# Moving the first k products forward in the first chunk of a q, k, v projection

## The chip, the cores and the metric

The kernel runs on one core of a Trainium2 chip. The metric is the device time of one execution in microseconds (us); the time before is the median of three runs, and the time after will be compared with it as a ratio. The engines are named as the profile names them: PE is TensorE (matmuls), PEld its weight loads, ACT is ScalarE, DVE is VectorE, POOL is GpSimd, and SP is SyncE, which here issues all the DMAs, one after the other.

## The reference

The inputs are a sequence x of 2048 tokens with 448 features, and weights. Everything is fp32. Cut to what matters:

```python
qkv = x @ wqkv                                # 448 -> 3 * 448, split into q, k, v of 16 heads x 28
# head h, position s: 8 keys at s, s-2, ..., s-14 (positions below 0 masked)
attn = softmax(q . k * 28**-0.5)              # over those 8
a = (attn . v) @ wo
b = relu(x @ w1 + b1)**2 @ w2 + b2            # 448 -> 1792 -> 448
g = sigmoid((x * gate_w).sum(-1))
out = g * a + (1 - g) * b
```

## The kernel before, in words

**Splitting for precision.** Every fp32 operand of a matmul is split into a high part (a rounded copy, made by ACT) and a low part (the operand minus the high part, made by DVE); `split_full` does both. A product then takes three matmuls: high x high, high x low, low x high. The q weights' parts are `wqh` and `wql`, which also hold the k and v weights in later columns.

**Row tiles.** The 448 features on the contracted side are three row tiles of 128 and a last one of 64. `full` lists the products of the row tiles named to it for one tile of 128 tokens; `last` lists those of the 64 rows. The last row tile of q and that of k lie in the two halves of one 128-row tile, `w7h`/`w7l`.

**Half-height pairs.** From `run` on, PE works in pairs: `side_by_side` (matmul at L186) issues two matmuls, one on array rows 0 to 63 and one on rows 64 to 127, for two different accumulators. A full product of 128 rows is thus issued once in each half, at different times. When an accumulator changes from one half to the other, `turn` puts a one-element write into its PSUM bank, on DVE (a 1x1 memset, L196) or, where one accumulator turns alone, on ACT (L194). PE waits for it before it goes on with that accumulator in the other half.

**Chunks.** The tokens come in four chunks of 512, each of four tiles of 128. The first chunk is done by `qkv_first`, the others by `qkv_two`, two token tiles at a time. In `qkv_first`, PE begins with q: for each of the three full row tiles in turn, twelve full-height matmuls (L255), four token tiles x three terms. Then comes the half-height part: q's last rows beside k's last rows, k's full row tiles, and then v. k's four accumulators take PSUM banks with the tag "m", those of q and then of v take banks with the tag "b".

**Loads at the start.** SP issues, in this order: for each row tile the q weights and the first chunk's tokens (tile `rx`; those of the first row tile in two halves), then the last row tile, then the three k weights, the three v weights, the last v rows (`raw7`), and the second chunk's tokens. These last take the buffer of the q weights, so they wait until DVE has copied the gate's weights out of it (L674). Thirteen matmuls on zeros (L634) run before the first tokens are there.

**Evacuation and storing.** `qkv_evacuate` (L205, ACT) copies an accumulator into a staging tile `st` that holds two token tiles; when both are in, SP stores it (L211) to `q_d`, `k_d` or `v_d` in HBM. The pool of staging tiles has three buffers (`ST_BUFS`). In the first chunk the first two hold q, the third and the fourth hold k, and the next two v.

**What sets the order.** The program is written once, with a planner's clock that stands for PE's time: each group of matmuls calls `advance` with an estimated cost (`MM448` = 203 ns for one matmul or one pair), and work registered with a due time is emitted at the first `advance` that passes it. In `run`, `advance` is called in steps of up to twelve pairs, and evacuations and turns are emitted behind it. Around the first chunk the due times are: storing the first chunk's split tokens to `x_d` (`x_spill`, four stores at L142) at 10,500; splitting the v weights at 12,000, 12,900, 13,800 and 14,700; the gate's partial products on DVE from 15,000; splitting the second chunk's tokens from 19,000. Each engine executes its instructions in the order in which they were emitted; only the waits between engines are settled at run time.

**Later.** From the second chunk on, attention runs on POOL and DVE beside PE's projections and then beside the two matmuls of the dense part.

Of the kernel before, what the change touches and what calls it, by code (L numbers as in the profile page):

```python
# [7 lines left out]
F32 = mybir.dt.float32  # L8
# [5 lines left out]
S, D, H, DH, W, F = 2048, 448, 16, 28, 8, 1792  # L14
P = 128
# [42 lines left out]
def gated_mix_kernel(ctx: ExitStack, tc: tile.TileContext, xT, wqkv, w1, w2, wo, b1, b2, out):  # L58
    nc = tc.nc

    def f32(ap):
        return ap.bitcast(F32)
# [30 lines left out]
    attp = ctx.enter_context(tc.tile_pool(name="attp", bufs=1))  # L93
# [20 lines left out]
    def split_full(raw, hi, lo, soon=now):  # L114
        nc.scalar.activation(hi, raw, AF.Copy)
        soon(lambda: nc.vector.tensor_sub(lo, raw, f32(hi)))

    def split_x78(raw, x7, x8, soon=now):

        split_full(raw, x7, x8, soon)  # L120
# [12 lines left out]
    def x_tiles(c, pool):  # L133
        return X([pool.tile([P, 2, CH], F32R, tag=f"x{j}", name=f"x{c}_{j}") for j in range(4)])
# [19 lines left out]
    wqh = ap.tile([P, 3, NP + 2 * D], F32R, name="wqh")  # L154
    wql = ap.tile([P, 3, NP + 2 * D], F32R, name="wql")
# [10 lines left out]
    def block(b):  # L166

        o = (0, NP, NP + D)[b]
        return slice(o, o + D)
# [43 lines left out]
    def full(x, acc, tl, b, ks=range(3)):  # L213
        sl, n = slice(tl * P, tl * P + P), block(b)
        r = []
        for k in ks:
            r += [(acc, x.h[k][:, sl], wqh[:, k, n]), (acc, x.h[k][:, sl], wql[:, k, n]),
                  (acc, x.l[k][:, sl], wqh[:, k, n])]
        return r

    def last(x, acc, tl, b):

        sl = slice(tl * P, tl * P + P)
        n = block(1) if b == 2 else slice(0, D)
        h, l = w7h[:, n], w7l[:, n]
        return [(acc, x.x7[:, sl], h), (acc, x.x7[:, sl], l), (acc, x.x8[:, sl], h)]

    def accs(c, b, tls, tags):
        return [Acc(t, f"qkv{c}_{tl}_{b}", D) for t, tl in zip(tags, tls)]

    def run(c, todo, steps):


        a = 0
        for e, done, *turns in steps:
            side_by_side(todo[0][a:e], todo[1][a:e])
            while a < e:
                advance(min(12, e - a) * MM448)
                a = min(a + 12, e)
            for t in turns:  # L240
                t() if callable(t) else turn(*t)
            for b, tl, acc in done:
                assert acc.todo == 0
                qkv_evacuate(acc.pt, c, tl, b)

    def qkv_first(x):


        four = range(4)
        q = accs(0, 0, four, "bbbb")  # L250
        for k in range(3):
            for two in ((0, 1), (2, 3)):
                for j, prods in enumerate(zip(*(full(x, q[i], i, 0, (k,)) for i in two))):
                    for acc, a, w in prods:
                        nc.tensor.matmul(acc.pt[:, :D], a, w, start=k == j == 0, stop=False)  # L255
            advance(12 * MM448)
        for acc in q:
            acc.todo = 3
        k = accs(0, 1, four, "mmmm")
        t = [sum((last(x, a[i], i, b) for i in four), []) for b, a in ((0, q), (1, k))]  # L260
        f = [full(x, k[i], i, 1) for i in four]
        run(0, [t[0] + f[0] + f[1] + f[2] + f[3], t[1] + f[2] + f[3] + f[0] + f[1]],
            [(3, [(0, 0, q[0])], (k[0], k[0])),
             (12, [(0, i, q[i]) for i in (1, 2, 3)], (k[1], k[1])),
             (24, [], (k[0], k[2])), (33, [], (k[1], k[3])),
             (39, [(1, 0, k[0]), (1, 2, k[2])]), (48, [(1, 1, k[1]), (1, 3, k[3])])])
        v = accs(0, 2, four, "bbbb")
        f, l = [full(x, v[i], i, 2) for i in four], [last(x, v[i], i, 2) for i in four]
        run(0, [f[0] + l[0] + f[2] + l[2] + f[1] + f[3], f[1] + l[1] + f[3] + l[3] + f[0] + f[2]],
            [(15, [], (v[0], v[1])), (24, [], (v[2], v[3])),  # L270
             (33, [(2, 0, v[0]), (2, 1, v[1])]), (42, [(2, 2, v[2]), (2, 3, v[3])])])
# [201 lines left out]
    def soon(fn):  # L473
        at(LO_DELAY, fn)

    def advance(dt):
        clock["pe"] += dt
        while due := [x for x in later if x[0] <= clock["pe"]]:
            item = min(due, key=lambda x: x[0])
            later.remove(item)  # L480
            item[1]()
        if not clock["on"]:
            clock["att"] = clock["pe"]
            return
        while clock["att"] < clock["pe"]:
            try:
                r = next(att)
            except StopIteration:
                clock["on"] = False
                return  # L490
            if r is None:
                clock["att"] = clock["pe"]
                return
            clock["att"] += r


    def raw_tile(name):
        return rawp.tile([P, 4, 512], F32, tag="raw", name=name)
# [94 lines left out]
    def h_first(x, c, f):  # L593

        accs = [Acc("m", f"h{c}_{f + r}", CH) for r in range(2)]
        go([h_last(x, a, f) + h_full(x, a, f + r, (0, 1, 2)) for r, a in enumerate(accs)], MM512)
        return accs
# [38 lines left out]

    raws = [raw_tile("wqraw0")]
    rx = raw_tile("xraw0")
    for k in range(4):
        if k < 3:  # L640
            nc.sync.dma_start(raws[0][:, k, :NQ], wqkv[0, :, k])
        else:
            for b, rows in ((0, slice(0, 64)), (1, slice(64, P))):
                nc.sync.dma_start(raws[0][rows, k, :NQ], wqkv[b, rows, k])
        for cols in ((slice(0, 256), slice(256, CH)) if k == 0 else (slice(0, CH),)):
            nc.sync.dma_start(rx[:, k, cols], xT[0, :, k, cols])

    for b, tag in ((1, "k"), (2, "v")):
        raw = attp.tile([P, 3, D], F32, tag=tag, name=f"wqraw{b}")
        for k in range(3):  # L650
            nc.sync.dma_start(raw[:, k], wqkv[b, :, k, :D])
        raws.append(raw)
    raw7 = attp.tile([P, D], F32, tag="q", name="wqraw7")
    nc.sync.dma_start(raw7, wqkv[2, :, 3, :D])
    x = x_tiles(0, xap)
    for k in range(3):
        nc.scalar.activation(wqh[:, k, :D], raws[0][:, k, :D], AF.Copy)
        halves = (slice(0, 256), slice(256, CH))
        for i, cols in enumerate(halves):

            if k == i == 0:
                nc.vector.tensor_copy(x.h[k][:, cols], rx[:, k, cols])
            else:
                nc.scalar.activation(x.h[k][:, cols], rx[:, k, cols], AF.Copy)
        nc.vector.tensor_sub(wql[:, k, :D], raws[0][:, k, :D], f32(wqh[:, k, :D]))
        for cols in halves:
            nc.vector.tensor_sub(x.l[k][:, cols], rx[:, k, cols], f32(x.h[k][:, cols]))
    split_full(raws[0][:, 3, :D], w7h[:, :D], w7l[:, :D])
    split_x78(rx[:, 3], x.x7, x.x8)

# [36 lines left out]
    def wq_split(b, k):  # L707
        if k < 3:
            split_full(raws[b][:, k], wqh[:, k, block(b)], wql[:, k, block(b)])
        else:  # L710
            split_full(raw7, w7h[:, NP:], w7l[:, NP:])
# [34 lines left out]
        nc.sync.dma_start(b1t, b1)  # L746
        nc.sync.dma_start(b2t, b2.partition_broadcast(P))

    for k in range(3):
        wq_split(1, k)  # L750
    for k in range(4):
        when(12000.0 + k * 900.0, wq_split, 2, k)
# [40 lines left out]
    for c in range(4):  # L793
        x = xs[c]
        if c == 0:
            qkv_first(x)
        else:
            qkv_two(x, c, 0, copies=c == 3)
            qkv_two(x, c, 2, (mlp_one, mlp_two) if c == 3 else (), c == 3)
        if c == 1:  # L800
            st_["spilled"] = 0
            clock["on"] = True
            clock["att"] = clock["pe"] - 1.0
            advance(0.0)
        if c == 3:
            st_["spilled"] = 1
# [282 lines left out]
    c, x = ORDER[0], xm[3]  # L1089
# [8 lines left out]
    for g in range(2, 2 * NF):  # L1098
        i, f = g // (NF // 2), g % (NF // 2) * 2
# [4 lines left out]
        if not f:  # L1104
            x, slots = X([nxt[j][0] for j in range(4)]), [nxt[j][1] for j in range(4)]
            nxt = {}
        hold[0] = ends
        accs = h_first(x, c, f)
# [112 lines left out]
```

## Time and profile before

| | us |
|---|---|
| time, median of 3 runs | 413.13 (412.95 to 413.48) |
| the profiled execution: time | 413.8 |
| the profiled execution: span, first to last instruction | 412.0 |
| PE busy | 407.8 |
| DVE busy | 270.6 |
| ACT busy | 210.4 |
| POOL busy | 268.4 |

The profile's page counts as busy the time in which an engine has an instruction in work. Matmuls are pipelined and their ends are modelled, so that two matmuls overlap in the rows and PE's real pace is read from start to start. A row of the timeline merges neighbouring instructions of one kind; its second column is then the time from the first start to the last end. Times of rows count from the span's start.

### The profile page before, as it was taken

The numbers are of one execution on the slowest core, as the hardware profiler recorded it, in microseconds if no ns is written. First come the engines' busy times: TensorE is split into PE (matmuls) and PEld (weight loads), VectorE is DVE, ScalarE is ACT, GpSimd is POOL, SyncE is SP. The second block draws the span as 40 slices with busy tenths as digits, with TensorE's granted clock in tenths as the row PEclk, the third lists the DMA queues.
The fourth block names the chain that finished last, engine by engine and source line by source line (L and its number), as shares of the span: only waits on it lengthen the run. The fifth ranks groups of instructions, "written<-read, shape, count | busy, mean of one in ns | idle before, by whom it ended". The sixth has DMA issues, their size and how long they took to land.

```text
span 412.0 us, 9331 instructions
## 1 busy us (share of the span) xinstructions
PE 407.8 (99%) x3835; PEld 366.0 (89%) x3835; DVE 270.6 (66%) x430; ACT 210.4 (51%) x461; POOL 268.4 (65%) x167
## 2 busy tenths in 40 slices
PE   8999999999999999999999999999999999999997
PEld 7999999999888888888888888989898888888996
DVE  4590745276767766787656798879576677892354
ACT  4641646387775555444565535444653254346540
POOL 0000001955999999989989899999899977940000
PEclk9999999999999999999999999999999999999999
DMA  7999999979262315654112649765146530168304
GB/s 213 368 351 309 286 390 288 355 223 315 91 241 99 128 51 209 208 186 152 41 47 105 222 158 270 196 146 154 28 157 200 217 130 2 45 179 132 95 0 181
DMA packets 66763, 73.83 MB, mean 179 GB/s; under 512 B 33120, under 2 KB 59296, under 8 KB 66464
## 3 DMA queue, kind: packets, MB, share of 16 engines
q1 hardware_dynamic: 66720, 73.23, 55.4%
q8 instruction: 30, 0.49, 0.5%
q14 instruction: 13, 0.11, 0.1%
HBM read 45.74 MB, written 28.28 MB: 180 GB/s over the span
## 4 chain that ended last, share of the span: by engine, by line
PE 99%; DVE 0%; issue 0%
PE b L186 33%; PE h L186 32%; PE qkv L186 23%; PE a L186 7%; PE qkv L255 2%; PE warm L634 1%; PE a L993 1%; PE last L993 0%; DVE bt L872 0%; PE last L985 0%; PE a L985 0%; DVE zero L631 0%; DVE b1z L632 0%
## 5 line engine op out<-in xcount | busy, mean ns | idle before, releaser
L335 POOL TENSOR_TENSOR qk<-q,k 128x896 f32<-128x896 f32 x64 | 135.2, 2144 | 84.2 <-DMA k<-k_d 76.0
L342 POOL TENSOR_TENSOR av<-lg,v 128x896 f32<-128x896 f32 x64 | 119.2, 1957 | 6.2 <-DVE lg L336 5.6
L621 DVE TENSOR_TENSOR h<-h,h 128x512 fp32r<-128x512 f32 x56 | 38.4, 688 | 66.8 <-ACT h L624 66.5
L186 PE MATMUL qkv<-wqh,x 64*128 64x448 f32 x528 | 78.2, 359 | 0.0
L336 DVE TENSOR_REDUCE lg<-qk 128x32 f32<-128x896 f32 x64 | 67.0, 1074 | 0.0
L350 DVE TENSOR_REDUCE o<-av 128x112 f32<-128x896 f32 x64 | 66.4, 1070 | 0.1
L186 PE MATMUL b<-w2ah,h 64*128 64x448 f32 x448 | 66.3, 359 | 0.0
L186 PE MATMUL b<-w2bh,h 64*128 64x448 f32 x448 | 66.1, 359 | 0.0
L622 ACT ACTIVATE h<-h,b1z 128x512 f32<-128x512 f32 x56 | 36.7, 655 | 43.6 <-PE h L186 43.6
L186 PEld LDWEIGHTS qkv<-wqh,x 64*128 64x128 f32 x528 | 49.4, 184 | 3.6
L186 PE MATMUL qkv<-wql,x 64*128 64x448 f32 x264 | 47.7, 358 | 0.0
L186 PEld LDWEIGHTS b<-w2bh,h 64*128 64x128 f32 x448 | 42.1, 184 | 3.5
L186 PEld LDWEIGHTS b<-w2ah,h 64*128 64x128 f32 x448 | 42.0, 184 | 3.7
L205 ACT ACTIVATE st<-qkv 128x448 f32<-128x448 f32 x48 | 23.5, 542 | 34.3 <-PE qkv L186 31.7
L186 PE MATMUL b<-w2bl,h 64*128 64x448 f32 x224 | 40.7, 358 | 0.0
L186 PE MATMUL b<-w2al,h 64*128 64x448 f32 x224 | 40.5, 358 | 0.0
L623 ACT ACTIVATE h<-h 128x512 fp32r<-128x512 f32 x56 | 33.5, 598 | 1.7
L624 ACT ACTIVATE h<-h 128x512 f32<-128x512 f32 x56 | 33.3, 594 | 0.0
L573 ACT ACTIVATE h<-h 128x4 fp32r<-128x4 f32 (+1 forms) x35 | 7.2, 207 | 44.4 <-PE b L186 44.2
L186 PE MATMUL h<-x2b,w1h 64*128 64x512 f32 x168 | 28.1, 386 | 0.0
L186 PE MATMUL h<-x,w1h 64*128 64x512 f32 x168 | 28.1, 386 | 0.0
L186 PE MATMUL h<-x1b,w1h 64*128 64x512 f32 x168 | 28.1, 386 | 0.0
(150 smaller groups left out, 688.6 us busy)
## 6 DMA issues: line engine op xcount, KB each, us to landing
k<-k_d SPq DMA_DIRECT2D x8, 840.0 KB, 5.6
v<-v_d SPq DMA_DIRECT2D x8, 840.0 KB, 5.0
x_d<-x SPq DMA_DIRECT2D x11, 512.0 KB, 6.8
q_d<-st SPq DMA_DIRECT2D x8, 448.0 KB, 5.5
k_d<-st SPq DMA_DIRECT2D x8, 448.0 KB, 5.2
v_d<-st SPq DMA_DIRECT2D x8, 448.0 KB, 5.8
w1raw<-w SPq DMA_DIRECT2D x4, 896.0 KB, 9.2
q<-q_d SPq DMA_DIRECT2D x8, 448.0 KB, 3.6
```

The costliest lines, as they stand in the source:

```text
L186: nc.tensor.matmul(acc.pt[:, :acc.n], a[rows], w[rows], start=acc.todo == acc.all, stop=acc.todo == 1)
L205: nc.scalar.activation(st[:, :, t % 2], pt[:, :D].rearrange("p (g c) -> p g c", g=G), AF.Copy)
L255: nc.tensor.matmul(acc.pt[:, :D], a, w, start=k == j == 0, stop=False)
L335: nc.gpsimd.tensor_mul(pr, q[:, s:s + 1].to_broadcast([P, W, C]), k[:, s:s + W])
L336: pending.append(lambda: nc.vector.tensor_reduce(lg[:, s], pr.rearrange("p w (h d) -> p w h d", h=HG), axis=AX.X, op=ALU.add))
L342: nc.gpsimd.tensor_mul(pr.rearrange("p (h d) w -> p w h d", h=HG), lg[:, s][:, :, :, None].to_broadcast([P, W, HG, DH]), v[:, s:s + W].rea ...
L350: nc.vector.tensor_reduce(o[:, g * C:(g + 1) * C], pr, axis=AX.X, op=ALU.add)
L573: nc.scalar.activation(ap, f32(ap), AF.Copy)
L621: nc.vector.tensor_sub(hl, pt, f32(hh))
L622: ops += [lambda pt=pt, r=r: nc.scalar.activation(pt, pt, AF.Relu, bias=b1t[:, f + r:f + r + 1]), lambda pt=pt, hh=hh: nc.scalar.activatio ...
L623: lambda pt=pt, hh=hh: nc.scalar.activation(hh, pt, AF.Square),
L624: lambda pt=pt, r=r, low=low: (nc.scalar.activation(pt, pt, AF.Square), at(delays[r], low))]
```

## The change

The first row tile of k is multiplied right behind the first row tile of q, at full height, by the loop that did q alone before. Its weights are loaded behind the first tokens and split behind the first tokens' low parts. The half-height part for k then does only row tiles 1 and 2, so that its pairs and the places of the evacuations and turns are counted anew: 36 pairs and not 48. The number of multiplications stays the same: twelve full-height matmuls take the place of twelve pairs. The k and v weights' buffers are declared earlier; the other loads keep their order among themselves.

```diff
         four = range(4)
-        q = accs(0, 0, four, "bbbb")
-        for k in range(3):
+        q, k = accs(0, 0, four, "bbbb"), accs(0, 1, four, "mmmm")
+        for b, n, acs in ((0, 0, q), (1, 0, k), (0, 1, q), (0, 2, q)):
             for two in ((0, 1), (2, 3)):
-                for j, prods in enumerate(zip(*(full(x, q[i], i, 0, (k,)) for i in two))):
+                for j, prods in enumerate(zip(*(full(x, acs[i], i, b, (n,)) for i in two))):
                     for acc, a, w in prods:
-                        nc.tensor.matmul(acc.pt[:, :D], a, w, start=k == j == 0, stop=False)
+                        nc.tensor.matmul(acc.pt[:, :D], a, w, start=n == j == 0, stop=False)
             advance(12 * MM448)
         for acc in q:
             acc.todo = 3
-        k = accs(0, 1, four, "mmmm")
+        for acc in k:
+            acc.todo = 15
         t = [sum((last(x, a[i], i, b) for i in four), []) for b, a in ((0, q), (1, k))]
-        f = [full(x, k[i], i, 1) for i in four]
+        f = [full(x, k[i], i, 1, (1, 2)) for i in four]
         run(0, [t[0] + f[0] + f[1] + f[2] + f[3], t[1] + f[2] + f[3] + f[0] + f[1]],
             [(3, [(0, 0, q[0])], (k[0], k[0])),
              (12, [(0, i, q[i]) for i in (1, 2, 3)], (k[1], k[1])),
-             (24, [], (k[0], k[2])), (33, [], (k[1], k[3])),
-             (39, [(1, 0, k[0]), (1, 2, k[2])]), (48, [(1, 1, k[1]), (1, 3, k[3])])])
+             (21, [], (k[0], k[2])), (27, [], (k[1], k[3])),
+             (30, [(1, 0, k[0]), (1, 2, k[2])]), (36, [(1, 1, k[1]), (1, 3, k[3])])])
...
     rx = raw_tile("xraw0")
+    raws += [attp.tile([P, 3, D], F32, tag=tag, name=f"wqraw{b}") for b, tag in ((1, "k"), (2, "v"))]
     for k in range(4):
...
             nc.sync.dma_start(rx[:, k, cols], xT[0, :, k, cols])
-
-    for b, tag in ((1, "k"), (2, "v")):
-        raw = attp.tile([P, 3, D], F32, tag=tag, name=f"wqraw{b}")
-        for k in range(3):
-            nc.sync.dma_start(raw[:, k], wqkv[b, :, k, :D])
-        raws.append(raw)
+        if k == 0:
+            nc.sync.dma_start(raws[1][:, 0], wqkv[1, :, 0, :D])
+
+    for b in (1, 2):
+        for k in range(b == 1, 3):
+            nc.sync.dma_start(raws[b][:, k], wqkv[b, :, k, :D])
...
             nc.vector.tensor_sub(x.l[k][:, cols], rx[:, k, cols], f32(x.h[k][:, cols]))
+        if k == 0:
+            split_full(raws[1][:, 0], wqh[:, 0, block(1)], wql[:, 0, block(1)])
...
-    for k in range(3):
+    for k in (1, 2):
         wq_split(1, k)
```

## The prediction

> **What bounds the kernel now.** First the page's busy times and the chain that ended last, then busy time by stretch (columns: stretch, sum of busy time, PE's busy time and instructions, granted clock, DMA share, GB/s).
>
> ```profile
> PE 407.8 (99%) x3835; PEld 366.0 (89%) x3835; DVE 270.6 (66%) x430; ACT 210.4 (51%) x461; POOL 268.4 (65%) x167
> ...
> 1.19 3.14 PE warm L634 x13
> 4.34 8.87 PE qkv L255 x36
> 13.21 91.55 PE qkv L186 x912
> ```
> ```profile
> 8.00:13.00 5.00, 5.00 (x26) 1.00 1.01 344
> 13.00:31.20 18.20, 18.20 (x182) 1.00 0.99 353
> 31.20:105.00 73.80, 73.80 (x740) 1.00 0.90 302
> 105.00:405.00 300.00, 300.00 (x2846) 1.00 0.44 135
> ```
>
> PE is the bound, and from 8 us to 405 us it shows no idle time at all. Two things follow. A microsecond for which PE is made to wait early on is not given back later, because there is no later wait in which it could vanish. And the change can only gain what PE loses before 13 us. That loss is read from the timeline's first matmuls (columns here and in all rows of this kind: start, time, engine, line, operation, tiles, count, and in brackets the idle time before and what ended it), from the weight loads (PEld) between them, and from the view of waits.
>
> ```profile
> 5.11 0.95 PE L255 MATMUL qkv<-wql,x 128*128 128x448 f32 x2
> 5.86 1.59 PE L255 MATMUL qkv<-wqh,x 128*128 128x448 f32 x4
> 7.29 0.56 PE L255 MATMUL qkv<-wql,x 128*128 128x448 f32 x2
> ...
> 9.84 0.56 PE L255 MATMUL qkv<-wql,x 128*128 128x448 f32 x2
> 10.25 0.96 PE L255 MATMUL qkv<-wqh,x 128*128 128x448 f32 x4
> 11.04 0.56 PE L255 MATMUL qkv<-wql,x 128*128 128x448 f32 x2
> ...
> 13.14 0.47 PE L186 MATMUL qkv<-w7h,x 64*128 64x448 f32 x2
> ```
> ```profile
> 8.13 0.30 PEld L255 LDWEIGHTS qkv<-wqh,x 128*128 128x128 f32 x2 [0.25 <-ACT x L664]
> ```
> ```profile
> PEld qkv L186 <- ACT wqh L115: 0.3, 1, 0.3
> PEld qkv L255 <- ACT x L664: 0.3, 1, 0.3
> ```
>
> In the steady part six full matmuls take 11.04 - 9.84 = 1.20 us, 0.20 us each. From 5.11 to 5.86 two of them take 0.75 us, 0.375 each, although the granted clock stands at 1.00. So of the 8.87 us of the 36 first matmuls, 36 x 0.20 = 7.2 are the work and 1.67 the loss, and most of the loss is the slow pace before 7.3 us, which the change does not touch. The one wait that more work from the first row tile can cover is the 0.25 to 0.3 us for the second tile's tokens (ACT x L664, at 8.1 us). The 0.3 at the switch to half-height matmuls (L186) stays.
>
> **The change, part by part.** *Matmuls.* Twelve full products of k (4 token tiles x 3 terms) come in behind the first 12 of q: 12 x 0.20 = 2.40 us. Out go 12 half-height pairs: 91.55 / 912 x 2 = 0.2008 us a pair, 2.41 us. Net zero. PE's own schedule becomes: half-height part from 13.14 - 0.2 + 2.4 = 15.35 us; after 36 pairs v's products; after 78 pairs the second chunk at 31.05, against 31.26 now (second pair of the last row below). That is a gain of 0.2 us, if nothing else waits.
>
> ```profile
> 30.86 0.36 PE L186 MATMUL qkv<-wql,x 64*128 64x448 f32 x2
> 31.06 0.56 PE L186 MATMUL qkv<-wqh,x 64*128 64x448 f32 x4
> ```
>
> *The first k weights.* One 224 KB transfer moves ahead of seven on SP's queue (q's second, third and last weights and the tokens between and behind them). It lands where q's second weights land today: ACT starts on those at 6.24, so k's are split at 6.24 + 0.58 = 6.8 on ACT and 0.6 later, 7.5, on DVE; PE wants them at 7.9.
>
> ```profile
> 5.62 0.42 ACT L664 ACTIVATE x<-xraw 128x256 fp32r<-128x256 f32 x1 [1.59 <-DMA xraw<-xT]
> 6.24 0.58 ACT L657 ACTIVATE wqh<-wqraw 128x448 fp32r<-128x448 f32 x1 [0.20 <-DMA wqraw<-wqkv]
> ```
>
> Those seven, and their splits, come 6.24 - 5.62 = 0.6 us later. PE now needs the second tile 2.4 us later, so all of that is covered; it would cost up to 0.6 without the new matmuls. Issue on SP (0.4 us) is not the limit, since the DMA share is about 1 already. The later k and v weights keep their place. The one follower that is not covered is the second chunk's tokens: their buffer comes free at DVE's copy of the gate's weights, now 12.0 + 0.16, then about 12.8, so they are issued and land up to 0.6 us later.
>
> ```profile
> 12.00 0.16 DVE L674 COPY zs<-wqraw 128x4 f32<-128x4 f32 x1
> ```
>
> *The queue's order, which the diff does not show.* The planner's clock reaches 10,500 ns, the due time of x_spill, in a different place. Today q's four tiles are evacuated by 9,744 (48 steps of 203) and the spill follows; changed, the first comes at 10,353 and the other three at 12,180 (60 steps), so before those three the spill's four x_d stores and one of v's weight splits are emitted first. On SP the four 512 KB x_d stores now stand ahead of the two q_d stores, and SP works strictly in order. The timeline of SP before:
>
> ```profile
> 15.34 1.45 SPq L211 DMA_DIRECT2D q_d<-st  x2
> 16.84 4.58 SPq L142 DMA_DIRECT2D x_d<-x  x4
> 23.64 0.99 SPq L211 DMA_DIRECT2D k_d<-st  x2
> ```
>
> Who waits for q_d: the pool of staging tiles has three buffers, and k's third tile (the fourth staging tile) takes the buffer of q's first. ACT's evacuation at about 21.7, second of the first row below, therefore waits until the first q_d store has landed. Today that is 15.34 + 5.5 = 20.8, under 1 us early. ACT's and DVE's rows of that stretch:
>
> ```profile
> 21.26 0.98 ACT L205 ACTIVATE st<-qkv 128x448 f32<-128x448 f32 x2 [3.00 <-PE qkv L186]
> 23.06 0.98 ACT L205 ACTIVATE st<-qkv 128x448 f32<-128x448 f32 x2 [0.82 <-PE qkv L186]
> 23.93 1.15 ACT L115 ACTIVATE x<-xraw 128x512 fp32r<-128x512 f32 x2
> ```
> ```profile
> 24.59 0.69 DVE L116 TENSOR_TENSOR x<-xraw,x 128x512 fp32r<-128x512 f32 x1 [0.18 <-ACT x L115]
> ...
> 26.28 0.06 DVE L196 MEMSET qkv<- 1x1 f32 x2
> ...
> 28.84 0.06 DVE L196 MEMSET qkv<- 1x1 f32 x2
> ```
>
> Landing of the changed order, call it T. The timeline's row of the last x_d store, and the view of DMA issues at 15.4, 20.8 and 23.8 us (tiles, count, KB, us from issue to landing):
>
> ```profile
> 20.35 1.07 SPq L142 DMA_DIRECT2D x_d<-x  x1
> ```
> ```profile
> q_d<-st SPq DMA_DIRECT2D x1, 448.0 KB, 5.5
> ```
> ```profile
> x_d<-x SPq DMA_DIRECT2D x1, 512.0 KB, 6.7
> ```
> ```profile
> k_d<-st SPq DMA_DIRECT2D x1, 448.0 KB, 4.8
> ```
>
> The last x_d lands at 20.35 + 6.7 = 27.05, and the k_d issued at 23.64 lands at 28.4, 1.35 behind it: stores land in the order of issue, one behind the other, at 0.99 DMA share. Exchanged, the four x_d and the first q_d have everything ahead of them that x_d's last has now, except the second q_d: T = 27.05 - 1.35 = 25.7, plus 0 to 0.6 for the later tokens. I take 25.9. The ends: q_d cannot be issued before its two evacuations are done, the second of which ends near 15.3 today (the row at 14.80 further below holds the second to the fourth) and then 2.2 later with PE and 0.5 more for v's split, at 18.0, and with the shortest landing, 4.8, T = 22.8; with the full 0.6 and half a store's spacing more, 0.7, T = 27.0. The row of x_d's last store is the same queue in the same microseconds, so the value lies at that end.
>
> What is queued behind the waiting evacuation on ACT: two more evacuations (start to start 0.44 each, from 23.06 to 23.93 for two), so three in 1.35, then the split of the second chunk's tokens. On DVE, in order behind that split, come the tokens' low halves and between them the two turns (the 1x1 memsets on L196) that v's products on PE wait for. From the split's start to the memsets it is 26.28 - 23.93 = 2.35 and 28.84 - 23.93 = 4.91. So:
> - first turn at T + 1.35 + 2.35 = T + 3.7 = 29.6. PE wants it at pair 60, 15.35 + 12.05 = 27.4: it stands 2.2 us.
> - PE resumes at 29.7, does 9 pairs (1.8) to 31.5, and wants the second turn, at T + 6.26 = 32.15: another 0.7.
> - 9 more pairs: the second chunk starts at 32.25 + 1.8 = 34.1, against 31.26: **+2.85 us**.
>
> The 0.2 gained and the smaller wait below are inside this, since T alone sets the end. That smaller wait: the turn of k's first two tiles on DVE now stands behind v's second and third weights, whose splits follow q's evacuations on ACT (16.29 today, some 2.5 later then): DVE reaches it at about 20.5, PE wants it at 15.35 + 24 x 0.2 = 20.2. It costs 0 to 0.4 by itself, and nothing when PE stands later anyway.
>
> ```profile
> 14.80 1.60 ACT L205 ACTIVATE st<-qkv 128x448 f32<-128x448 f32 x3
> 16.29 1.50 ACT L115 ACTIVATE wqh<-wqraw 128x448 fp32r<-128x448 f32 x3
> ```
>
> *Behind 34 us* everything follows PE's order: ACT is done with the tokens by T + 3.6, v's first evacuation needs the second q_d (T + 1.35), the k_d stores land about T + 5, before PE's end of v. I cost that at nothing; the cover is 3 us.
>
> Sum: the profiled execution took 413.8 (span 412.0 and 1.8 around it); changed, 413.8 + 2.85 = 416.65. The median of the runs is 413.13, 0.67 under the profiled one, so 416.0.
>
> **The clock, row against rule.** The two matmuls at 0.375 us show half pace at the start with a granted clock of 1.00. The Trainium skill, "TensorE: Matmul & The Clock Gate", Part 1, says that the array runs at half rate until it has been busy for a window of about 3.4 us, and falls back after an idle window of that length. The early slow pace agrees in kind. By that page the stop of 2.2 us is too short to matter; an estimate from its window would add about 1.7 us where it isn't.
>
> **The rivals.**
> *Not slower.* A q_d store needs 4.8 to 5.5 us whatever is ahead of it. It decides at T = 27.4 - 3.7 = 23.7: at or below, the first turn is in time. Then the sum is -0.2 + 0.4 at most for k's turn, 413.1 to 413.3. For it: those are the medians of the page's stores. Against: x_d takes 6.7 in the same queue, and k_d lands only behind it. Chance 0.09.
> *A small loss.* T from 23.7 to 24.5, when ACT is done early and the queue drains faster: the end is T + 8.2, so up to 32.7, +1.4: 413.4 to 414.6. Chance 0.08.
> *PE falls back to half pace in the stop.* For it: the early matmuls at 0.375, double the later 0.20, after a slow start. At half pace PE loses half of each microsecond; a stretch of 3 us, half of the six that the slow pace lasts at the start (1.2 to 7.3), loses 1.5: 417.5. Against: the stop is 2.2 us, with work before it. Chance 0.08.
> *Faster.* The change does what it says, covers the wait at 8.1 us, and no queue intervenes: -0.25 at most, 0.06%, which is not to be told from none. More would need the slow pace to end earlier. Chance of over 0.2%: 0.02.
> *It doesn't cover the wait.* If k's first weights land over 0.4 us later than reckoned, PE stands at 7.9 for them instead. That shifts PE by up to 0.6 and still leaves T as the limit; it is inside the forecast.
>
> **The numbers.** Forecast, T from 24.5 to 27.0: 0.73, own range 414.6 to 417.1 (T + 8.2 - 31.26 from 1.44 to 3.94). Below it lie 0.09 + 0.08 + 0.02, above it 0.08. Leaving out most of the not-slower case below, and reaching to the clock's case above, gives 413.5 to 417.7. A difference of 0.2% (0.83 us) is about what a measurement of this kernel can tell from none: faster 0.02; same 0.10 (the not-slower case and the lowest part of the small loss); slower 0.88.
>
> **What the changed profile would show.** Right: no wait of the weight loads at 8 us; x_d issued ahead of q_d on SP; ACT's evacuation into the fourth staging tile waiting 3 to 5 us for a q_d landing at 25 to 27; the memsets on DVE near 29.6 and 32; PE standing near 27.5 to 29.6 and again near 31.5; every later stage some 3 us late and unchanged in itself. Wrong: q_d landing by 23.7 though issued last; or PE without a wait between 20 and 34; or a later stage that takes the 3 us back.

## The result, and the profile after

The changed kernel takes 418.35 us (median of 4 runs, 417.98 to 419.03) against 413.04 for the kernel before (4 runs, 412.95 to 413.48): ratio 1.0128 [1.0111, 1.0146]. It is 5.3 us slower, in the direction predicted, and 0.65 us above the upper end of the predicted range. The profiled execution took 418.65 us with a span of 416.8.

The busy times on the page of the changed kernel, and then two steps of the chain that ended last, in order of time (columns: start, time, engine, group):

```profile
PE 409.3 (98%) x3823; PEld 395.2 (95%) x3823; DVE 270.4 (65%) x430; ACT 210.7 (51%) x461; POOL 269.0 (65%) x167
```
```profile
4.34 10.47 PE qkv L255 x48
...
18.70 7.90 DMA q_d<-st
```

PE's 48 full-height matmuls stand where 36 stood. What is new is that the chain leaves PE: for 7.9 us it goes through the landing of a q_d store. The path from there back to PE is read from SP, the DMA issues of 18.8 us (tiles, count, KB, us to landing), ACT, DVE and PE, all of the changed kernel:

```profile
12.81 1.75 SPq L566 DMA_DIRECT2D xraw<-xT  x4
14.61 4.00 SPq L142 DMA_DIRECT2D x_d<-x  x4
18.70 2.09 SPq L211 DMA_DIRECT2D q_d<-st  x2
```
```profile
q_d<-st SPq DMA_DIRECT2D x1, 448.0 KB, 7.9
```
```profile
21.45 0.55 ACT L205 ACTIVATE st<-qkv 128x448 f32<-128x448 f32 x1 [1.90 <-PE qkv L186]
26.70 1.42 ACT L205 ACTIVATE st<-qkv 128x448 f32<-128x448 f32 x3 [4.70 <-DMA q_d<-st]
```
```profile
28.67 0.69 DVE L116 TENSOR_TENSOR x<-xraw,x 128x512 fp32r<-128x512 f32 x1 [4.06 <-ACT x L115]
...
30.35 0.06 DVE L196 MEMSET qkv<- 1x1 f32 x2
...
32.91 0.06 DVE L196 MEMSET qkv<- 1x1 f32 x2
```
```profile
27.05 0.36 PE L186 MATMUL qkv<-w7h,x 64*128 64x448 f32 x2
30.49 0.47 PE L186 MATMUL qkv<-wqh,x 64*128 64x448 f32 x2 [3.08 <-DVE qkv L196]
...
33.59 0.57 PE L186 MATMUL qkv<-wql,x 64*128 64x448 f32 x2
33.96 0.95 PE L186 MATMUL qkv<-wqh,x 64*128 64x448 f32 x4
34.71 0.57 PE L186 MATMUL qkv<-wql,x 64*128 64x448 f32 x2
...
35.84 0.57 PE L186 MATMUL qkv<-wqh,x 64*128 64x448 f32 x4
```

The four x_d stores now stand ahead of q_d. The first q_d store lands at 18.70 + 7.9 = 26.6, ACT's fourth evacuation waits 4.70 us for it, DVE waits 4.06 us for the split of the second chunk's tokens, which stands behind that evacuation on ACT, DVE's two turns come at 30.35 and 32.91, and PE starts again at 30.49. From 33.59 to 34.71 three pairs take 1.12 us, 0.373 each, where 0.20 is the normal pace. The second pair of the row at 35.84 begins the second chunk, at 36.04. It began at 31.26 before: 4.78 us later, which is all of the 416.8 - 412.0 = 4.8 by which the span grew.

The slow pairs have a granted clock of one half. Busy time by stretch of the changed kernel, the stretches cut where the granted clock falls and rises and at equal distances ahead of it (columns: stretch, length, then busy time and count for PE, PEld, DVE, ACT and POOL, then granted clock, DMA share, GB/s):

```profile
25.17:28.58 3.41, 2.24 (x24) 1.75 (x20) 0.00 (x0) 1.88 (x5) 0.00 (x0) 1.00 0.32 110
28.58:31.99 3.41, 1.50 (x14) 1.42 (x16) 3.32 (x8) 1.61 (x4) 0.00 (x0) 1.00 1.04 308
31.99:35.40 3.41, 3.32 (x18) 2.46 (x17) 2.99 (x7) 0.98 (x2) 0.00 (x0) 0.50 0.84 316
35.40:38.81 3.41, 3.41 (x36) 3.27 (x36) 0.09 (x2) 0.98 (x2) 0.00 (x0) 1.00 1.02 385
...
105.00:405.00 300.00, 300.00 (x2846) 292.58 (x2844) 210.40 (x283) 154.68 (x342) 248.51 (x145) 1.00 0.44 137
```

Exactly one stretch of 3.41 us runs at half clock, from 31.99, when PE had been back at work for 1.5 us: 18 matmuls in it, 36 in the next. All four runs have a mean granted clock of 0.995 or 0.996, so this is not of the profiled execution alone. Behind the stretch the clock is whole again, and PE is busy without a gap and does 2846 matmuls from 105 to 405 us, the number of the kernel before. Nothing is given back and nothing more is lost.

### The profile page after: what moved, and what is told of

Its sections match the earlier page's. It is cut to its first block, busy times and chain, and to the rows that moved or that the text cites. A ratio compares the mean times of both kernels' runs of the same rounds, so it can differ in the third digit from the quotient of the medians.

```text
span 416.8 us, 9307 instructions
## 1 busy us (share of the span) xinstructions
PE 409.3 (98%) x3823; PEld 395.2 (95%) x3823; DVE 270.4 (65%) x430; ACT 210.7 (51%) x461; POOL 269.0 (65%) x167
## 4 chain that ended last, share of the span: by engine, by line
PE 95%; DMA 2%; ACT 1%; DVE 1%; issue 1%; ACTq 0%
PE b L186 32%; PE h L186 32%; PE qkv L186 19%; PE a L186 7%; PE qkv L255 3%; DMA q_d<-st 2%; PE warm L635 1%; PE a L997 1%; ACT st L205 1%; ACT wqh L115 0%; PE last L997 0%; DVE zu L684 0%; DVE x L116 0%; ACT x L115 0%; PE a L989 0%
## 5 line engine op out<-in xcount | busy, mean ns | idle before, releaser
L186 PE MATMUL b<-w2ah,h 64*128 64x448 f32 x448 | 69.8, 359 | 0.0
L186 PE MATMUL b<-w2bh,h 64*128 64x448 f32 x448 | 69.5, 359 | 0.0
L186 PEld LDWEIGHTS qkv<-wqh,x 64*128 64x128 f32 x512 | 50.9, 187 | 6.4 <-DVE qkv L196 4.7
L186 PEld LDWEIGHTS b<-w2ah,h 64*128 64x128 f32 x448 | 46.7, 184 | 0.4
L186 PEld LDWEIGHTS b<-w2bh,h 64*128 64x128 f32 x448 | 46.7, 184 | 0.4
L186 PE MATMUL b<-w2bl,h 64*128 64x448 f32 x224 | 43.5, 358 | 0.0
L186 PE MATMUL b<-w2al,h 64*128 64x448 f32 x224 | 43.5, 358 | 0.0
L186 PE MATMUL h<-x,w1h 64*128 64x512 f32 x168 | 29.6, 386 | 0.0
L186 PE MATMUL h<-x0b,w1h 64*128 64x512 f32 x168 | 29.6, 386 | 0.0
L186 PE MATMUL h<-x1b,w1h 64*128 64x512 f32 x168 | 29.6, 386 | 0.0
```

What stands on the lines that cost most here:

```text
L186: nc.tensor.matmul(acc.pt[:, :acc.n], a[rows], w[rows], start=acc.todo == acc.all, stop=acc.todo == 1)
```

## The experiments

### Where the loss starts

**The stores back behind q's.** In the changed kernel only the due time of the x_d stores moves.

```diff
-    when(10500.0, x_spill, 0, x)
+    when(12500.0, x_spill, 0, x)
```

> The changed kernel, with one due time set back so that the planner emits the four x_d stores behind the two q_d stores again, as before the change; the k products, their loads and the v split's place stay as changed. Theory (the loss comes from q_d behind x_d in SP's queue, which ACT, DVE and PE then wait for): q_d is issued near 17.4 us and lands near 22.5, ACT's evacuation into the fourth staging tile waits at most 1 us, PE does not stand at 27 us and keeps full pace: 412.8 to 413.6. Rival (the loss comes from the k products or their loads themselves): 416 or more.

Measured: 413.75 us against 413.33, ratio 1.0011 [1.0002, 1.0021]. SP, the DMA issue of 17.49 us and PE's wait for turns in this kernel:

```profile
17.49 1.87 SPq L211 DMA_DIRECT2D q_d<-st  x2
19.41 3.91 SPq L142 DMA_DIRECT2D x_d<-x  x4
```
```profile
q_d<-st SPq DMA_DIRECT2D x1, 448.0 KB, 3.5
```
```profile
PEld qkv L186 <- DVE qkv L196: 0.5, 1, 0.5
```

With q_d ahead of x_d it lands 3.5 us after its issue, at 21.0, no evacuation waits for it, and 4.9 of the 5.3 us are gone, although k's products are still moved. So nearly all of the loss hangs on the order of these stores and not on the moved products.

**Another buffer for the fourth staging tile.** In the changed kernel the staging tile that would take q's first buffer is taken from another pool. SP's order stays as it is.

```diff
+            if (c, b, tl) == (0, 1, 2):
+                own = prodp.tile([P, W * C], F32, tag="pp", name="st_own", bufs=PP_BUFS)
+                stage[b, t // 2] = own.rearrange("p (g s c) -> p g s c", g=G, s=2)
+            else:
...
```

> The changed kernel with x_d still ahead of q_d, but k's third and fourth token tiles in the first chunk are staged in a buffer of another pool, so that nobody waits for the first q_d store before v is evacuated. Theory: q_d lands as late as in the changed kernel, 26 to 27, ACT does not wait for it, PE does not stand at 27 us: 412.8 to 413.6. Rival (the late stores or the crowded DMA queues slow something else down as well): 415 or more.

Measured: 413.77 against 413.33, 1.0012 [1.0003, 1.0021]. ACT, the DMA issue of 19.1 us and PE's wait:

```profile
21.96 0.54 ACT L209 ACTIVATE st_own<-qkv 128x448 f32<-128x448 f32 x1
```
```profile
q_d<-st SPq DMA_DIRECT2D x1, 448.0 KB, 8.5
```
```profile
PEld qkv L186 <- DVE qkv L196: 0.5, 1, 0.5
```

The store is as late as ever, 8.5 us after its issue, at 27.6. The evacuation into `st_own` runs at 21.96 without a wait, and the time is that of the run above. A late store by itself costs nothing here (the two medians differ by 0.02 us); the loss needs the shared buffer, which ties ACT, then DVE's turns, then PE to its landing.

**The early stores alone.** The kernel before, k's products unmoved, with the due time put ahead of q's evacuations.

```diff
-    when(10500.0, x_spill, 0, x)
+    when(9000.0, x_spill, 0, x)
```

> The kernel before, with nothing of the change, but the due time of the x_d stores set to 9,000 so that they stand ahead of the q_d stores. Theory: q_d lands at 25.5 to 26.6, the first turn of v comes at 29.2 to 30.4 where PE wants it at 27.5, PE stands 1.7 to 2.9 us there and 0.7 us more at the second turn: 415.5 to 416.6, and 1.5 more if the stop makes the clock fall. Rival (the order of the stores matters only with the k products moved): 413.0.

Measured: 418.02 against 413.33, 1.0104 [1.0088, 1.0120]; the four runs are 418.07, 416.46, 418.10 and 417.98. ACT, PE's waits and the stretches of this kernel:

```profile
26.41 1.42 ACT L205 ACTIVATE st<-qkv 128x448 f32<-128x448 f32 x3 [4.67 <-DMA q_d<-st]
```
```profile
PEld qkv L186 <- DVE qkv L196: 3.1, 2, 2.8
```
```profile
27.78:31.19 3.41, 1.00 (x10) 0.94 (x12) 2.83 (x7) 2.11 (x5) 0.00 (x0) 1.00 0.83 261
31.19:34.60 3.41, 3.41 (x22) 2.85 (x20) 3.34 (x8) 0.98 (x2) 0.00 (x0) 0.50 0.90 323
```

One due time, with no product moved, reproduces the loss: the same wait of 4.7 us on ACT, the same stop, the same stretch at half clock. The run of 416.46 is 3.1 us above the median before, as much as PE's waits of 3.1 alone; its mean granted clock is 0.999, where one stretch at half clock makes 0.996 (3.41 x 0.5 of 416 us is 0.4%). Two of the others have 0.995 and 0.996 and are 1.6 us longer. The fourth, 417.98 at a mean of 1.000, does not fit this and has no profile.

### What the half clock needs, and what it costs

Four kernels are the one before with a delay put on DVE ahead of the first turn of v, and nothing else: n memsets that write zeros to a tile that holds zeros. They add idle time to PE without any change of the queues.

```diff
+    def delay(n):
+        for _ in range(n):
+            nc.vector.memset(f32(zero), 0.0)
...
-            [(15, [], (v[0], v[1])), (24, [], (v[2], v[3])),
+            [(15, [], lambda: delay(14), (v[0], v[1])), (24, [], (v[2], v[3])),
```

The number here is 14; the other kernels have 20, 6 and 9.

> The kernel before with fourteen idle memsets (128x256) on DVE ahead of v's first turn, which make PE stop there though no store and no buffer is touched. Each should take 0.21 to 0.27 us, 2.9 to 3.8 in all, of which 1.3 are slack: a stop of 1.7 to 2.5 us and 0.7 more at the second turn. Theory (PE falls to half pace when a stop is about 3 us long, and not below): the granted clock stays at 1.00 and the time is 415.7 to 416.6. Rival (any stop of PE over a microsecond or two does it): the granted clock at 0.5 for some 3 us and 417.2 or more.

> The same with twenty memsets: a stop of 2.9 to 4.1 us and 0.7 at the second turn. Theory: the granted clock falls to 0.5 behind the stop for some 3 us, which costs 1.5 us on top of 3.7 to 4.9: 418.5 to 419.8. Rival (the fall of the clock in the changed kernel has to do with the crowded DMA or with the late stores): 417.0 to 418.2 and a granted clock of 1.00.

> The kernel before with six idle memsets ahead of v's first turn. They took 0.38 us each in the run with fourteen, so 2.3 us less 1.1 of slack: PE stops for about 1.2 us and 0.7 at the second turn, 1.9 in all. Theory (the granted clock is judged over stretches of 3.41 us whose phase differs from run to run, and falls when PE was idle for more than half of one): no stretch is idle for more than 1.7 us in most runs, the clock stays at 1.00: 415.1 to 415.6 in most. Rival (any such stop makes it fall): 416.8 or more.

> The same with nine memsets: a stop of 2.3 us and 0.7 at the second turn. Theory: whether a stretch holds more than 1.7 us of the stop depends on the phase of the run, so the runs fall into two kinds, without the fall at 416.2 to 416.8 and with it 1.7 us later, at 417.9 to 418.5, and the profile's clock rows tell which kind it is. Rival (the length of the stop alone decides): all runs of one kind.

The memsets took longer than reckoned (14 in 5.36 us, 0.38 each), so the stops with 14 and 20 came out at 4.3 and 6.7 us, longer than the one in question; the runs with 6 and 9 were made to close that gap. "Waits" is the sum of PE's waits for the turns:

| memsets | waits, us | time, us (against) | loss beyond the waits, us | mean granted clock of the runs |
|---|---|---|---|---|
| 6 | 2.1 | 415.32 (413.41) | 1.9 - 2.1 = -0.2 | 0.999 to 1.000 |
| 9, two runs | 3.2 | 416.28, 416.37 (413.41) | 2.9 - 3.2 = -0.3 | 1.000 |
| 9, one run | 3.2 | 417.43 (413.41) | 4.0 - 3.2 = 0.8 | 0.996 |
| 14 | 4.3 | 420.03 (413.48) | 6.55 - 4.3 = 2.2 (runs: 1.3 to 3.4) | 0.992 to 0.996 |
| 20 | 6.7 | 422.20 (413.48) | 8.7 - 6.7 = 2.0 | 0.991 to 0.992 |

The ratios are 1.0040 [1.0027, 1.0053], 1.0082 [1.0053, 1.0112] with all four runs of nine, 1.0163 [1.0138, 1.0188] and 1.0205 [1.0189, 1.0221]. The waits are those of each profiled execution. The stretches, first with 14 and then with 20, 9 and 6 memsets:

```profile
28.46:31.87 3.41, 0.67 (x6) 0.64 (x8) 2.69 (x11) 0.00 (x0) 0.00 (x0) 1.00 0.66 261
31.87:35.28 3.41, 3.41 (x22) 3.08 (x20) 3.34 (x8) 0.79 (x2) 0.00 (x0) 0.50 0.04 12
```
```profile
28.86:32.27 3.41, 0.00 (x0) 0.00 (x0) 2.45 (x9) 0.00 (x0) 0.00 (x0) 1.00 0.47 190
32.27:35.68 3.41, 1.71 (x10) 1.55 (x12) 2.93 (x9) 0.00 (x0) 0.00 (x0) 0.50 0.00 0
35.68:39.09 3.41, 3.41 (x22) 3.05 (x20) 2.78 (x7) 0.98 (x2) 0.00 (x0) 0.50 0.02 5
```
```profile
27.58:30.99 3.41, 2.02 (x22) 1.54 (x18) 2.57 (x9) 0.31 (x1) 0.00 (x0) 1.00 1.03 318
30.99:34.41 3.42, 2.33 (x20) 1.86 (x22) 3.30 (x11) 0.64 (x2) 0.00 (x0) 1.00 0.42 172
```
```profile
27.31:30.73 3.42, 2.26 (x20) 1.61 (x18) 3.18 (x10) 0.24 (x1) 0.00 (x0) 1.00 0.89 327
```

A stop on PE alone, with no store ahead of another, brings the clock down. The DMA share of 0.04 with 14 memsets and 0.00 and 0.02 with 20 shows that the half clock does not need busy queues. Where the mean clock shows no such stretch, the runs with 6 and the two short ones with 9 lose the length of the stop and no more; where it does, 0.8 to 3.4 us come on top. One stretch at half clock can cost at most half of 3.41 us, 1.7; the run of 421.15, at a mean of 0.996, lost 1.7 more than that, and no profile shows where. With nine memsets two bands of times were expected: two runs lie in the first, 417.43 lies between them, and 418.65, above both, shows no half clock.

The stretches above are cut at whole multiples of 3.41 us behind the end of the slow start of each execution; the last section shows why. Cut so, they part by how long PE is busy in one of them: with 1.50 (the changed kernel), 1.00, 0.67 and 0.00 the next stretch is at half clock, with 2.02, 2.26 and 2.33, and with the 2.24 of the changed kernel's stretch from 25.17, it is not. With 20 memsets a stretch of 1.71, itself at half clock, is followed by another at half. The limit would lie somewhere between 1.50 and 2.02. This fits every stretch listed, but it is not shown that the busy time in a stretch decides and not the length of the stop: with nine memsets the longest wait of 2.4 us lay across two stretches, and the waits behind which the clock fell were 2.8 us and longer. No run puts one and the same stop once inside a stretch and once across two.

The profiled execution with nine memsets took 418.65 us without a stretch of granted half clock. Its start accounts for some 1.5 of the 2.3 us by which it is longer than the two shortest, if these began as the kernel before did: the slow pace, 0.37 a matmul, lasted until 10.3 us, against 7.3 in the kernel before, and 3 us at half pace lose 1.5.

```profile
8.82 1.70 PE L259 MATMUL qkv<-wqh,x 128*128 128x448 f32 x4
10.31 0.67 PE L259 MATMUL qkv<-wql,x 128*128 128x448 f32 x2
10.82 0.97 PE L259 MATMUL qkv<-wqh,x 128*128 128x448 f32 x4
```

### What the change is worth without the stop

With the stores' order repaired, 0.4 us of loss remain, and PE still waits 0.5 us for k's first turn at 20 us. Three kernels move v's weight splits away from that turn; the first two keep the stores late as above, the third keeps the extra staging buffer.

```diff
-        when(12000.0 + k * 900.0, wq_split, 2, k)
+        when(12500.0 + k * 900.0, wq_split, 2, k)
```

> As the run with the later spill, and the splits of the v weights set back by 500 ns of the planner's clock, so that they too stand behind q's evacuations, as before the change. Theory: the 0.5 us for which PE stood at 19.9 us for the turn of k's first tiles goes too; what is left of the change is the wait of 0.25 us at 8.1 us that it covers: 412.5 to 413.1. Rival (that wait was hidden): the same time as with the later spill alone.

Measured: 414.07 against 413.33, 1.0019 [1.0009, 1.0028]: not the gain expected.

```diff
-        when(12000.0 + k * 900.0, wq_split, 2, k)
+        when((14010.0, 14020.0, 15300.0, 15310.0)[k], wq_split, 2, k)
```

> The changed kernel with the x_d stores behind the q_d stores and v's weight splits emitted behind the turn of k's first tiles on DVE, so that neither the stop at 27 us nor the one of 0.5 us at 20 us should be left. Theory: this is the change by itself, the 0.2 to 0.3 us of the covered wait against the 0.6 us later loads: 413.0 to 413.4, within 0.1% of before and 0.3 to 0.5 faster than the run with the later spill alone. Rival (the stop at 20 us was hidden, or something else takes its place): 413.75 as there.

Measured: 414.49 against 413.48, 1.0019 [1.0010, 1.0028]. PE's waits for turns, first of the kernel with 12500 and then of this one:

```profile
PEld qkv L186 <- DVE qkv L196: 0.9, 3, 0.4
```
```profile
PEld qkv L186 <- DVE qkv L196: 1.2, 2, 0.9
```

Pushed back, the splits delay later turns: the waits are 0.9 in three places, then 1.2 us in two, no longer 0.5 in one. Moved ahead instead:

```diff
-        when(12000.0 + k * 900.0, wq_split, 2, k)
+        when((11000.0, 11010.0, 11020.0, 14700.0)[k], wq_split, 2, k)
```

> The changed kernel with the buffer from another pool for k's third and fourth token tiles, and with three of v's weight splits moved ahead of q's later evacuations, so that DVE reaches the turn of k's first tiles in time. Theory: neither the stop at 27 us nor that at 20 us is left, and this time the work on DVE behind it is not later than before: 413.1 to 413.5, against 413.77 with the buffer alone. Rival (the 0.5 us at 20 us is lost in another wait, as it was when v's splits were moved behind the turn): 413.7 or more.

Measured: 413.67 against 413.41, 1.0002 [0.9988, 1.0016]. The wait shrinks to 0.3:

```profile
PEld qkv L186 <- DVE qkv L196: 0.3, 1, 0.3
```

This is the best version with k's products moved, and it is not to be told from the kernel before. **Only the loads moved**, the last of these, is the kernel before with k's first weights loaded and split early, while PE's order stays the old one:

```diff
+        if k == 0:
+            nc.sync.dma_start(raws[1][:, 0], wqkv[1, :, 0, :D])
...
+        if k == 0:
+            split_full(raws[1][:, 0], wqh[:, 0, block(1)], wql[:, 0, block(1)])
...
-    for k in range(3):
+    for k in (1, 2):
```

> The kernel before with one part of the change alone: k's first weights are loaded and split in the changed place, while PE's order and the planner's clock stay as before. Theory: the loads behind it come 0.6 us later and PE waits for the second row tile's tokens, up to 0.6 us more than before; the stores keep their order and nothing stands at 27 us: 413.3 to 414.0. Rival (the moved load is free): 413.3, and no longer wait before 9 us.

Measured: 414.17 against 413.48, 1.0020 [1.0009, 1.0031], 0.7 us. In its profile PE starts later and waits at the first matmuls, not at the second row tile; the kernels with 9 and 14 memsets, whose loads were not moved, wait 0.9 us at the first matmuls as well. So the start differs between executions, this one profile does not show where the 0.7 us are lost, and that stays open.

## Why the prediction was right about the place and wrong about the size

*The queue's order and the chain of waits: right.* x_d went ahead of q_d, the store held the fourth staging tile, and ACT, DVE and PE followed in that order. The first of the three store experiments undoes the order, the second cuts the chain at the buffer, the third sets it off alone. The working from T onward held to 0.1 us: first turn 30.35 - 26.6 = T + 3.75 (reckoned 3.7), second turn T + 6.3 (6.26), PE 0.14 behind the turn.

*T: 0.7 us too early.* The step that failed is "T = 27.05 - 1.35 = 25.7, plus 0 to 0.6 for the later tokens. I take 25.9". It takes over the pace of the queue from the kernel before. Busy time of 14 to 18 us, in the kernel before and then the changed one (stretch, length, PE's busy time and instructions, granted clock, DMA share, GB/s):

```profile
14.00:18.00 4.00, 4.00 (x44) 1.00 1.02 352
```
```profile
14.00:18.00 4.00, 4.00 (x36) 1.00 0.80 218
```

The queue moved 218 GB/s where it had moved 352. The last of the second chunk's token loads by the DMA issues of 13.6 us (kernel before), 14.1 (changed) and 14.0 (changed, stores back behind q's):

```profile
xraw<-xT SPq DMA_DIRECT2D x1, 256.0 KB, 4.7
```
```profile
xraw<-xT SPq DMA_DIRECT2D x1, 256.0 KB, 5.7
```
```profile
xraw<-xT SPq DMA_DIRECT2D x1, 256.0 KB, 5.6
```

Issued at 13.57 it landed at 18.25; now, issued at 14.13, it lands at 19.85. The tokens are 1.6 us later and not 0 to 0.6: their issue moved by 0.6 as reckoned, and the load itself took 1.0 longer. That the x_d stores slow it, the first of which is now issued 0.5 us behind it (14.61), is not shown: with the stores back the next store came 3.5 us behind it, at 17.49, and it took 5.6 us all the same. Nor do the moved loads make T late by themselves: in the early-stores kernel, where no load was moved, ACT's evacuation began at 26.41, against 26.70 here. Why the queue moved less stays open. The landing at 26.6 was inside the bounds given, 22.8 to 27.0.

*The clock: the rival that came true on top.* The failed step is "Against: the stop is 2.2 us, with work before it", by which the fall of the pace was left out of the sum. The reckoning for the second chunk was T + 8.2 = 34.1; it came at 36.04, 1.94 later. Of these T has 0.7, PE's resumption 0.1, and the rest, 1.15, is the half-clock stretch: half of 3.41 is 1.7, of which some 0.5 fell into the wait for the second turn, that PE would have had anyway. That is the mechanism of the rival given 0.08, and its price of 1.5 was near. The stop was longer than reckoned, 27.25 to 30.49 = 3.2 us: 0.7 by T, 0.2 because the turn came 0.05 later behind T and PE 0.14 behind the turn, and 0.15 because PE arrived at 27.25 and not at 27.4 (the half-height part began at 14.73 instead of 15.35, for the slow pace ended near 4.9 us in this execution, but 0.5 of that went into the wait at k's turn). The length of the stop was a narrow ground to leave the clock out: by the view of waits the one of 2.4 us with nine memsets did not bring it down, the one of 2.8 us in the early-stores kernel did, as did the 3.4 us here, and the reckoning allowed T 2.5 us of room. Nor is a stretch without any work needed, as the prediction took it: PE was busy for 1.50 us of the one ahead of the fall.

*The sum.* Against the profiled executions 2.85 were predicted and 4.85 measured, of which 1.94 are the two steps above. The medians differ by a further 0.4, because the prediction took the 0.67 by which the median before lay under its profiled execution to hold for the changed kernel too, and there it is 418.65 - 418.35 = 0.3.

*The gain of 0.2 and k's turn.* The wait at 8.1 us is gone, as said, but two others came in its place, and k's turn cost what was given as its upper end and a little more. Weight loads of the changed kernel:

```profile
5.84 0.30 PEld L255 LDWEIGHTS qkv<-wqh,x 128*128 128x128 f32 x2 [0.34 <-ACT x L666]
...
7.72 0.30 PEld L255 LDWEIGHTS qkv<-wql,x 128*128 128x128 f32 x2 [0.36 <-DVE wql L116]
...
19.94 0.19 PEld L186 LDWEIGHTS qkv<-wqh,x 64*128 64x128 f32 x2 [0.50 <-DVE qkv L196]
```

The first of these is for the second half of the first tokens, which the change does not move; PE came to it early in this execution. The second is the case named under "It doesn't cover the wait", though the weights were hardly late: their low half was ready at 7.7, 0.2 us later than reckoned, and PE was there at 7.36 and not at 7.9. With the stop removed, the medians show +0.4 us in two kernels, 0.7 and 1.0 in those with v's splits set back, and 0.26 us, within the measurement, in the last: no version shows the gain.

*Behind 34 us: right.* The later stages are unchanged, only later.

## What to carry to other kernels

When work moves along a planner's clock, follow everything with a due time near it, and then each queue in its new order: here four stores that nobody touched overtook two others, and a buffer that was shared with them carried the delay to PE. A late store costs nothing until a buffer's next user waits for it, so count the buffers between the store and the engine that bounds the kernel. A stop of some 2 to 3 us on a saturated PE should be priced at its length and, as a second outcome with a real chance, at its length plus about 1 to 2 us of half clock; here neither of the two alone explains the loss.

## What was not expected of the hardware

**The clock changes on a grid of fixed stretches.** In the changed kernel the slow pace at the start ends near 4.9 us:

```profile
4.19 0.88 PE L255 MATMUL qkv<-wqh,x 128*128 128x448 f32 x2
4.91 0.56 PE L255 MATMUL qkv<-wql,x 128*128 128x448 f32 x2
5.31 1.21 PE L255 MATMUL qkv<-wqh,x 128*128 128x448 f32 x4
```

Two matmuls take 0.72 us from 4.19, the next two 0.40. Eight stretches of 3.41 us behind 4.7 to 4.9 lie 32.0 to 32.2, and the clock fell at 31.99. The early-stores kernel and those with 14 and 20 memsets fit the same way: slow pace until 7.3, 4.6 and 5.0 us, and the clock down at 31.19 (seven stretches on), 31.87 and 32.27 (eight). The traces' own records of the granted clock are sharper: in these four they begin at 4.69, 7.30, 4.56 and 4.96 us, and the fall is recorded 27.307, 23.893, 27.307 and 27.307 us later, which is 8, 7, 8 and 8 times 3.413. In all thirteen kept traces each recorded period, but for the last, which the trace cuts off, is a whole multiple of 3.413 us long. Before the first record the granted clock reads 1.00 in the rows although the pace is half. So the time of the fall is set by a grid that each execution begins at another place, and it comes when PE has been working again for 1.0 us (early stores) or 1.5 us (changed kernel). This would also explain why the same kernel falls in one run and not in another; no kernel was profiled both ways. The Trainium skill, "TensorE: Matmul & The Clock Gate", Part 1, has the free-running window of about 3.4 us, and the stretches of 3.41 agree. It asks for an idle window before the clock falls; here a window with PE busy for 1.50 of 3.41 us was enough, so for a partly idle window the measurement decides against that reading.

**A store's landing depends on what is ahead of it.** The same 448 KB q_d store took 3.5 us (stores late), 5.5 (kernel before), 7.9 (changed kernel) and 8.5 (fourth tile). Taking one figure for a kind of transfer, as the not-slower rival did, would have missed the whole loss.
